# A bridge between two stages: the first expert's last tokens go through their first product between the steps of the earlier tokens' second product

## The chip, the cores and the metric

The kernel runs on 1 core of one Trainium2 chip. The metric is the device time of one execution in microseconds; less is better. Three timed runs of the kernel before gave a median of 729.29 us (727.39 to 729.51).

## What is computed

Attention with a cluster mask (4 batches, 8 heads, 768 positions, head size 64), and then a mixture of 16 experts (4 groups of 4) over the 3072 tokens of 512 features. Cut to what matters:

```python
def _attn_ref(q, k, v, centroids):
    q_assign = np.argmax(np.einsum('bhsd,hcd->bhsc', q_n, c_n), axis=-1)
    k_assign = np.argmax(np.einsum('bhsd,hcd->bhsc', k_n, c_n), axis=-1)
    mask = q_assign[:, :, :, None] == k_assign[:, :, None, :]
    scores = np.where(mask, scale * np.matmul(q, k.transpose(0, 1, 3, 2)), -1e9)
    ...
    return np.matmul(attn, v)

def _moe_ref(x, w_group, w_expert, w1, w2):
    g_idx = np.argmax(x @ w_group, axis=1)
    ...
            e_idx = np.argmax(xg @ w_expert[g], axis=1)
            ...
            h = np.maximum(xg[mask_e] @ w1[g, e], 0.0)
            ye = h @ w2[g, e]
            out[tok_idx] = combined[:, None] * ye
```

Every expert multiplies its tokens by `w1` (512 x 1024), applies ReLU and multiplies by `w2` (1024 x 512). These are called the first and the second product.

## The kernel before

Values are kept as two fp16 halves, a high one and a low one (names ending in h and l), so that each product is three matmuls: high by high, high by low, low by high.

**Attention** runs batch after batch. The router picks an expert for the tokens of a batch when its attention is done (`Router.decide`), and GpSimd scatters each token's number and weight into a table in DRAM (`table`, L713), six scatters of 128 rows a batch.

**Experts** run in order of their number of tokens. The expert that leads after three batches is "the first expert"; its weights are fetched and split while attention still runs (`WA`). Its tokens come in two parts. Part A, up to 288 tokens of the first three batches, is gathered and transposed during the last heads (`xTA`), and is computed by the generator `ga` (`part_a`): 8 steps of the first product, then 8 steps of the second, each of 12 matmuls of 288 columns. Part B, up to 128 tokens of the last batch, is known only after the last `decide`. Beside A's steps the kernel

- makes the tables of the last batch on VectorE (`slots_new`, a generator in several steps, whose one-hot rows `oS` lie in a tile named `hh`; its last step, `widths`, makes `wi`, two words that say which experts may run with fewer columns),
- picks B's rows out of the attention output by a product with a one-hot matrix (`tokens_b`, L1288 and L1292; the result is `xT`, evicted by VectorE and ScalarE at L1289),
- computes every expert's list of token numbers and weights with two groups of matmuls (`slots`, L1306 and L1312), copies them to `ri` and `rg` (L1142, L1143), and starts the first gathers: GpSimd fetches rows of `xbuf` by `ri` into `xg` (L995), three gathers for the next expert, and three for the one behind it that follow at once on GpSimd's queue.

Then `ranks` runs one round for each expert, `k = -1, 0, 1, ...`. Round `k` interleaves, in 8 steps, the first product of expert `k` with the second product of the one before. Round -1 is B's first product (L1036, 128 columns), with nothing of a second product beside it, since A's is over by then. In its middle the tokens of expert 0 are transposed on TensorE (`tokens`, L1005, evicted to `xT` at L1007), and A's result is turned back and written (`settle`, L1114 and L1127, scatter L1128).

**Weights** of the later experts stream in by SyncE in chunks of 512 KB (`st`, L810). A chunk is split in two steps: ScalarE (later by turns GpSimd) makes the high half (L817, `wh..`), VectorE the low half (L820, `wl..`). `next(self.fill)` takes one chunk a step. A chunk's buffer comes free, and the next load can start, when its low half is made.

**Order.** Rounds 0 to 14 are traced in a block with a bound order (`manual_schedule(engines=PINNED)`): TensorE, ScalarE and VectorE execute in the order in which the code is written. Everything ahead of them, round -1 too, is ordered by the scheduler, with `issue_after` as a hint. Part of the code before:

```python
    for i, _ in enumerate(ga):
        with tc.issue_after(X.mm.ins):
            if i >= X.ADD:
                next(new, None)
            if i == X.SLOTS:
                X.slots()
            if i == X.SLT:
                X.xTB = X.tokens_b()
```

PSUM banks: three for the first product (`psh`), two for the second (`psy`), three for everything else (`psm`). A PSUM tile's bank comes free when its eviction is done: `hh` by ScalarE (L1040) and `hl` by VectorE (L1041) for a `psh` tile, `yh` (L1070) and `yl` (L1071) for a `psy` tile of A.

## Time and profile before

| | |
|---|---|
| median of 3 runs | 729.29 us (727.39 to 729.51) |
| profiled execution | 725.85 us, of which the span is 724.1 us |
| TensorE (PE) busy | 690.4 us, 95% of the span |
| VectorE (DVE) busy | 594.9 us, 82% |
| GpSimd (POOL) busy | 498.1 us, 69% |
| ScalarE (ACT) busy | 478.3 us, 66% |
| mean granted TensorE clock | 0.990 |

The span runs from the first to the last instruction of one profiled execution. Attention takes the time up to about 391 us, the stretch that the change rewrites lies between 404.5 and 440.0 us, and the rounds of the later experts follow. PE is matmuls, PEld weight loads, which overlap them. A row of the timeline gives start, duration, engine, line, operation, output and inputs, count, and in brackets the idle time of the engine just before with what ended it. "remote" there means a semaphore whose writer the profile could not name at that moment, "issue" that the row shows no wait.

### The profile page before, as it was taken

To read this page: it belongs to the slowest core of one execution; us is meant where nothing else is said; L and a number is where in the kernel's file an instruction comes from. 1 tells how busy PE (TensorE), PEld (TensorE's weight loads), DVE (VectorE), ACT (ScalarE), POOL (GpSimd) and SP (SyncE) were. 2 spreads that over 40 slices of the span, in tenths; PEclk is the share of its full clock that TensorE was granted. 3 is DMA by queue.
4 is the path that set the end of the run, shared out by engine and by line. 5 is a ranking of instruction groups with operands and counts; after the bars stand their busy time and mean duration, and the time that the engine had idled before them with its cause. 6 is when DMAs were issued, how large, how long until landed. Compare 5 with 4: busy or idle time off the path is not lost.

```text
span 724.1 us, 26359 instructions
## 1 busy us (share of the span) xinstructions
PE 690.4 (95%) x10520; PEld 587.5 (81%) x10520; DVE 594.9 (82%) x1228; ACT 478.3 (66%) x921; POOL 498.1 (69%) x538
## 2 busy tenths in 40 slices
PE   5889999999999999999999979999999999999996
PEld 3667888887788878878778767888779989999996
DVE  5999989899898998989896737878678787999961
ACT  5658798897988979887994246545444554555542
POOL 9777898889988899889973333644645464665433
PEclk9999999999999999999999989999999999999998
DMA  9866727558275573633835468887979797889831
GB/s 252 203 171 170 205 73 200 133 125 196 75 202 135 133 187 80 135 90 78 202 74 106 76 196 316 291 221 240 323 238 309 256 306 248 293 285 318 289 103 51
DMA packets 91848, 137.27 MB, mean 190 GB/s; under 512 B 43815, under 2 KB 61735, under 8 KB 91704
## 3 DMA queue, kind: packets, MB, share of 16 engines
q1 hardware_dynamic: 85948, 121.81, 60.2%
q0 software_dynamic: 5600, 13.40, 5.3%
q8 instruction: 103, 1.69, 1.0%
q14 instruction: 41, 0.34, 0.2%
q10 hardware_dynamic: 156, 0.03, 0.0%
HBM read 93.25 MB, written 14.11 MB: 148 GB/s over the span
## 4 chain that ended last, share of the span: by engine, by line
PE 69%; DVE 12%; ACT 8%; issue 5%; DMA 3%; POOL 1%; another core or an unknown queue 1%; SPq 1%; POOLq 0%; DVEq 0%; ACTq 0%
PE psh L1036 19%; PE psy L1064 14%; PE pso L394 9%; PE psc L320 6%; PE psf L362 5%; PE psf L363 5%; DVE mpart L323 5%; PE psy L1088 4%; ACT p L367 3%; PE psm L253 2%; PE psm L1114 2%; PE psm L1005 1%; ACT ph L371 1%; DMA qx<-xbuf,idA 1%; PE psm L632 1%
## 5 line engine op out<-in xcount | busy, mean ns | idle before, releaser
L374 POOL TENSOR_TENSOR pl<-p 128x512 f16<-128x512 f32 x193 | 198.3, 1052 | 19.5 <-ACT p L367 17.1
L323 DVE TENSOR_REDUCE mpart<-psc 128x1 f32<-128x512 f32 (+1 forms) x282 | 188.2, 680 | 17.5 <-PE psc L320 15.7
L367 ACT ACTIVATE p<-psf 128x512 f32<-128x512 f32 x288 | 171.6, 599 | 40.6 <-PE psf L363 31.0
L394 PE MATMUL pso<-V,pl 128*128 128x65 f16 (+1 forms) x1968 | 160.7, 193 | 0.0
L362 PE MATMUL psf<-A 82*128 82x384 f16 (+2 forms) x576 | 143.7, 274 | 2.4 <-ACT p L367 0.8
L363 PE MATMUL psf<-B 128*128 128x384 f16 (+2 forms) x576 | 143.6, 274 | 0.0
L394 PEld LDWEIGHTS <-pl 128*128 128x128 f16 x1968 | 130.8, 97 | 1.9 <-issue 0.4
L394 PEld LDWEIGHTS <-p 128*128 128x128 bf16 x1632 | 112.5, 98 | 20.3 <-issue 0.5
L394 PE MATMUL pso<-V,p 128*128 128x65 f16 x1632 | 120.8, 193 | 0.0
L374 POOL TENSOR_TENSOR pl<-p,ph 128x512 f16<-128x512 f32 x84 | 96.7, 1160 | 24.8 <-POOL pl L374 9.5
L320 PE MATMUL psc<-A 80*128 80x512 f16 (+1 forms) x376 | 106.8, 328 | 4.6 <-DVE mpart L323 3.2
L1040 ACT ACTIVATE hh<-psh 128x160 f16<-128x160 f32 (+14 forms) x136 | 47.1, 346 | 88.4 <-PE psh L1036 78.6
L1041 DVE SCALAR_TENSOR_TENSOR hl<-psh,hh 128x160 f16<-128x160 f32 (+14 forms) x136 | 50.4, 371 | 54.2 <-ACT hh L1040 44.1
L995 POOL DMA_INDIRECT xg<-xbuf,ri x32 | 37.3, 1167 | 57.0 <-PE psm L1005 28.9
L1036 PE MATMUL psh<-xT,wh0a 128*128 128x288 f16 (+12 forms) x512 | 69.2, 247 | 1.3 <-DVE yl L1071 1.2
L363 PEld LDWEIGHTS <-B 128*128 128x128 f16 x576 | 56.8, 99 | 13.8 <-issue 4.2
L362 PEld LDWEIGHTS <-A 82*128 82x128 f16 x576 | 56.0, 98 | 9.5 <-issue 0.9
L1036 PE MATMUL psh<-xT,wh0b 128*128 128x272 f16 (+6 forms) x448 | 60.7, 247 | 0.1
L1036 PE MATMUL psh<-xT,wl0a 128*128 128x288 f16 (+7 forms) x256 | 60.1, 246 | 0.3 <-issue 0.3
L1128 POOL DMA_INDIRECT out_dram<-y,ri x32 | 36.7, 1148 | 24.7 <-ACT y L1127 17.7
L1036 PE MATMUL psh<-xT,wl0b 128*128 128x248 f16 (+6 forms) x224 | 53.7, 246 | 0.0
L371 ACT CAST ph<-p 128x512 f16<-128x512 f32 x84 | 51.9, 617 | 2.3
(316 smaller groups left out, 1650.9 us busy)
## 6 DMA issues: line engine op xcount, KB each, us to landing
st<-w SPq DMA_DIRECT2D x128, 512.0 KB
B<-parts SPq DMA_DIRECT2D x64, 192.0 KB
kx<-kT SPq DMA_DIRECT2D x16, 384.0 KB
qx<-qT SPq DMA_DIRECT2D x16, 384.0 KB
vx<-vr SPq DMA_DIRECT2D x16, 384.0 KB
A<-parts SPq DMA_DIRECT2D x32, 192.0 KB
xbuf<-xs SPq DMA_DIRECT2D x16, 384.0 KB
A<-mk SPq DMA_DIRECT2D x56, 24.0 KB
```

Source lines behind the costliest of these rows:

```text
L320: last["mm"] = nc.tensor.matmul(out=pc[:, off:off + k1 - k0], lhsT=QA[h % 8][0:80, c * P:(c + 1) * P], rhs=KA[h % 8][0:80, k0:k1], start=T ...
L323: nc.vector.tensor_reduce(out=(mp[:, 0, 0:1], mp[:, :, 1], mp[:, 1, 0:1])[i], in_=pc.rearrange("p (a x) -> p a x", a=n), axis=AX.X, op=ALU ...
L362: nc.tensor.matmul(out=o, lhsT=KA[h % 8][0:82, ks], rhs=QA[h % 8][0:82, q0:q1], start=True, stop=False)
L363: nc.tensor.matmul(out=o, lhsT=KBs[h][:, ks], rhs=QBs[h][:, q0:q1], start=False, stop=True)
L367: cfg["exp"] = nc.scalar.activation(out=p32, in_=pf, func=AF.Exp, scale=QK / (SQ * SQ))
L371: nc.scalar.copy(out=ph, in_=p32)
L374: lo = (nc.vector if u in (EARLY if h < 2 else DVE_LO[h % 8] if h < NH - 2 else DVE_END[h - NH]) else nc.gpsimd).tensor_tensor(out=pl, in0 ...
L394: nc.tensor.matmul(out=O[:, col:col + v.shape[-1]], lhsT=p[:, bs], rhs=v, start=c == 0 and q == 0 and i == 0, stop=c == NCH - 1 and i == l ...
L1036: self.mm = nc.tensor.matmul(out=ph[:, 0:n], lhsT=w[:, k, fs], rhs=xT[:, a, k, 0:n], start=i == 0, stop=i == 3 * KD - 1)
L1040: nc.scalar.activation(out=hh[:, f], in_=ph[:, 0:M], func=AF.Relu)
L1041: self.ev = nc.vector.scalar_tensor_tensor(out=hl[:, f], in0=ph[:, 0:M], scalar=0.0, in1=hh[:, f], op0=ALU.max, op1=ALU.subtract)
L1064: self.mm = nc.tensor.matmul(out=py[:, 0:n], lhsT=w[:, f, d * P:(d + 1) * P], rhs=a[:, f, 0:n], start=i == 0, stop=i == len(prods) - 1)
```

## The change

A new method `bridge` takes the place of the loop above and of round -1. A's 8 steps of the first product run as before. From the second product on, everything is traced inside a bound block:

- `tokens_b` comes after A's first step of the second product (it was after its fifth), `slots` after its third (it was after its sixth).
- B's first product has its 8 steps spread by `BESIDE`: of A's eight steps of the second product, counted from 0, steps 1, 3, 4, 5, 6 and 7 are each followed by one step of B's, and the last two of B's stand behind the transposes of expert 0's tokens.
- A's results are turned back (`settle`) at the very end of the bridge, behind B's last step.
- one weight chunk is taken with each step from `slots` on, eight in all, as many as before.
- `oS` lies in the memory of `wh1b`, the not yet filled high half of expert 0's second weights, and no longer in a tile named `hh`.
- `ranks` starts at round 0 with the state that `bridge` returns.

The core of the diff:

```diff
-    SLOTS = 13
-    SLT = 12
+    SLOTS = 2
+    BESIDE = 0, 1, 0, 1, 1, 1, 1, 1
...
-        self.oS = self.xp.tile([P, T, max(self.caps)], F16, name="hh")
+        n = T * max(self.caps)
+        self.oS = self.W[1][1][0].rearrange("p f d -> p (f d)")[:, 0:n].rearrange("p (t x) -> p t x", t=T)
...
+    def bridge(self, ga, new):
+
+        for i in range(8):
+            next(ga)
+            with self.tc.issue_after(self.mm.ins):
+                if i >= self.ADD:
+                    next(new, None)
+        self.pinned = True
+        with self.tc.manual_schedule(engines=PINNED):
+            h = []
+            up = None
+            for i in range(8):
+                next(ga)
+                if self.left:
+                    self.left()
+                    self.left = None
+                for _ in range((2, 1, 0, 1)[i] if i < 4 else 0):
+                    next(new, None)
+                if i == 0:
+                    self.xTB = self.tokens_b()
+                    up = self.up(self.xTB, P, self.WA[0:2], h)
+                for _ in range(self.BESIDE[i]):
+                    next(up)
+                if i == self.SLOTS:
+                    self.slots()
+                if i >= self.SLOTS:
+                    next(self.fill)
+            for _ in ga:
+                pass
+            xT = self.tokens(self.xg0, self.caps[0])
+            for _ in up:
+                next(self.fill)
+            self.settle()
+        return xT, self.xg0, None, self.down(h, P, self.WA[2:4], [self.gB], [self.idB])
...
-                for _ in range((1, 1, 1, 0, 0, 2, 2, 1)[i] if k < 0 else 1):
-                    with ExitStack() as order:
-                        for op in (self.kept, self.turned, self.got, self.yev[min(1 + i, 3)], self.ev) if k < 0 else (self.ev,):
-                            order.enter_context(self.tc.issue_after(op.ins))
-                        next(self.fill, None)
+                with self.tc.issue_after(self.ev.ins):
+                    next(self.fill, None)
...
-        state = round_(-1, xT, xgs, nxt, down)
-        self.pinned = True
...
+    state = X.bridge(ga, X.slots_new())
```

How the change moves instructions is seen at three places. Lines behind L940 have numbers lower by 1 in the changed kernel up to L1208, so L1041 there is L1040.

**ScalarE, from A's second product on.** `yh` (128x288) evicts a tile of A's second product, `hh` (128x128) one of B's first product, `wh0a` and `wh0b` are weight chunks of experts 0 and 1. Before:

```order
L1070 ACTIVATE yh<-psy 128x288 x2
L1289 CAST xT<-psm 128x512
L817 ACTIVATE wh0a<-st 128x2x512
L1070 ACTIVATE yh<-psy 128x288
L817 ACTIVATE wh0a<-st 128x2x512
L1070 ACTIVATE yh<-psy 128x288
L817 ACTIVATE wh0a<-st 128x2x512
L1040 ACTIVATE hh<-psh 128x128
L817 ACTIVATE wh0a<-st 128x2x512
L1040 ACTIVATE hh<-psh 128x128 x2
```

Of the change:

```order
L1289 CAST xT<-psm 128x512
L1069 ACTIVATE yh<-psy 128x288
L1039 ACTIVATE hh<-psh 128x128
L817 ACTIVATE wh0a<-st 128x2x512
L1069 ACTIVATE yh<-psy 128x288
L1039 ACTIVATE hh<-psh 128x128
L817 ACTIVATE wh0a<-st 128x2x512
L1039 ACTIVATE hh<-psh 128x128
L817 ACTIVATE wh0a<-st 128x2x512
L1069 ACTIVATE yh<-psy 128x288
L1039 ACTIVATE hh<-psh 128x128
```

The four evictions of A's second product stood ahead of all of B's; now they stand between them, and `tokens_b`'s eviction is the first of all.

**VectorE, ahead of expert 0's tokens.** `hl` (128x128) evicts B's first product, `wl..` are the low halves of weight chunks, `xT` (128x4x128) are expert 0's transposed tokens. Before:

```order
L820 SCALAR_TENSOR_TENSOR wl0a<-st,wh0a 128x2x512
L1041 SCALAR_TENSOR_TENSOR hl<-psh,hh 128x128 x3
L1007 COPY xT<-psm 128x4x128 x2
L1007 COPY xT<-psm 128x4x32
L820 SCALAR_TENSOR_TENSOR wl0a<-st,wh0a 128x2x512
```

Of the change:

```order
L1040 SCALAR_TENSOR_TENSOR hl<-psh,hh 128x128
L820 SCALAR_TENSOR_TENSOR wl0a<-st,wh0a 128x2x512
L1070 SCALAR_TENSOR_TENSOR yl<-psy,yh 128x288
L1040 SCALAR_TENSOR_TENSOR hl<-psh,hh 128x128
L820 SCALAR_TENSOR_TENSOR wl0a<-st,wh0a 128x2x512
L1040 SCALAR_TENSOR_TENSOR hl<-psh,hh 128x128
L820 SCALAR_TENSOR_TENSOR wl0a<-st,wh0a 128x2x512
L1070 SCALAR_TENSOR_TENSOR yl<-psy,yh 128x288
L1040 SCALAR_TENSOR_TENSOR hl<-psh,hh 128x128
L820 SCALAR_TENSOR_TENSOR wl0b<-st,wh0b 128x2x512
L1006 COPY xT<-psm 128x4x128 x2
L1006 COPY xT<-psm 128x4x32
```

Three low halves of chunks stood ahead of the token copies before; now five do, and a chunk's low half stands right ahead of them.

**TensorE, where the two words of `wi` are read.** `TENSOR_LOAD wi` reads a word into a register of TensorE's sequencer. Before, the first load stood between two steps of B's first product (`wh`, `wl` are `WA`):

```order
L1036 LDWEIGHTS wl_9368
L1036 MATMUL psh<-xT,wl_9368 128x128
L1256 TENSOR_LOAD wi
L1256 ISA x2
L1036 LDWEIGHTS wh_9367
L1036 MATMUL psh<-xT,wh_9367 128x128
```

Of the change, between `settle` (`psm<-back`) and expert 0's first product (`wh0a`):

```order
L1113 LDWEIGHTS yl
L1113 MATMUL psm<-back,yl 32x128
L1256 TENSOR_LOAD wi
L1256 ISA x2
L1256 TENSOR_LOAD wi
L1256 ISA x2
L1267 REGISTER_ALU
L1267 COMPARE_AND_BRANCH
L1035 LDWEIGHTS wh0a
L1035 MATMUL psh<-xT,wh0a 128x288
```

Both loads stand together now, between the last matmul of the bridge and the first of round 0.

## Rows read from the trace of the kernel before

**Rows 1.** The page's first part: busy time of each engine.

```profile
PE 690.4 (95%) x10520; PEld 587.5 (81%) x10520; DVE 594.9 (82%) x1228; ACT 478.3 (66%) x921; POOL 498.1 (69%) x538
```

**Rows 2.** By stretch: length; PE, PEld, DVE, ACT, POOL (instructions); granted clock; DMA share; GB/s.

```profile
404.50:440.00 35.50, 30.32 (x369) 26.10 (x367) 18.08 (x57) 14.48 (x27) 13.62 (x13) 0.90 0.66 176
425.20:431.80 6.60, 2.76 (x48) 2.59 (x46) 2.23 (x5) 2.74 (x5) 3.95 (x5) 0.87 0.69 228
431.80:437.00 5.20, 5.00 (x50) 4.50 (x50) 4.03 (x9) 4.31 (x8) 0.96 (x1) 0.50 0.52 160
```

**Rows 3.** Timeline of TensorE's matmuls: start, duration, engine, line, operation, names, count, idle.

```profile
407.16 1.14 PE L1064 MATMUL psy<-hl,wh 128*128 128x288 f16 x8
...
412.00 1.14 PE L1064 MATMUL psy<-hh,wh 128*128 128x288 f16 x8 [0.56 <-DVE yl L1071]
...
426.31 0.22 PE L1036 MATMUL psh<-xT,wl 128*128 128x128 f16 x1
...
431.85 0.37 PE L1036 MATMUL psh<-xT,wh 128*128 128x128 f16 x2 [3.89 <-issue]
...
433.44 0.39 PE L1036 MATMUL psh<-xT,wh 128*128 128x128 f16 x2 [0.16 <-issue]
...
440.00 0.42 PE L1036 MATMUL psh<-xT,wh0a 128*128 128x288 f16 x2
```

**Rows 4.** Timeline of ScalarE.

```profile
411.05 0.84 ACT L1070 ACTIVATE yh<-psy 128x288 f16<-128x288 f32 x2 [5.04 <-remote]
...
431.19 0.28 ACT L1040 ACTIVATE hh<-psh 128x128 f16<-128x128 f32 x1 [3.50 <-remote]
...
436.25 0.59 ACT L1007 COPY xT<-psm 128x512 f16<-128x512 f16 x1
```

**Rows 5.** Timeline of GpSimd: the last table scatter of six, and three gathers of six.

```profile
409.29 0.96 POOL L713 DMA_INDIRECT table<-pay,rdi  x1 [0.30 <-issue]
423.26 0.98 POOL L995 DMA_INDIRECT xg<-xbuf,ri  x1 [13.02 <-issue]
...
427.01 0.95 POOL L995 DMA_INDIRECT xg<-xbuf,ri  x1 [0.31 <-issue]
...
429.51 0.86 POOL L995 DMA_INDIRECT xg<-xbuf,ri  x1 [0.30 <-issue]
```

**Rows 6.** The chain that ended last, 380 to 450 us: start, duration, what.

```profile
422.14 3.05 PE psy L1064 x24
...
438.02 1.45 PE psm L1114 x24
```

**Rows 7.** Timeline of VectorE.

```profile
422.18 0.21 DVE L1142 CAST ri<-psm 128x48 int32<-128x48 f32 x1 [2.15 <-PE psm L1312]
...
425.67 0.46 DVE L1071 SCALAR_TENSOR_TENSOR yl<-psy,yh 128x288 f16<-128x288 f32 x1 [3.17 <-ACT yh L1070]
...
426.99 1.27 DVE L820 SCALAR_TENSOR_TENSOR wl0a<-st,wh0a 128x1024 f16<-128x1024 f32 x1
...
431.71 1.22 DVE L820 SCALAR_TENSOR_TENSOR wl0a<-st,wh0a 128x1024 f16<-128x1024 f32 x1
432.85 0.28 DVE L1041 SCALAR_TENSOR_TENSOR hl<-psh,hh 128x128 f16<-128x128 f32 x1
433.05 1.22 DVE L820 SCALAR_TENSOR_TENSOR wl0a<-st,wh0a 128x1024 f16<-128x1024 f32 x1
...
435.79 0.43 DVE L1007 COPY xT<-psm 128x512 f16<-128x512 f16 x1 [0.25 <-PE psm L1005]
```

**Rows 8.** Line L1256 on TensorE's sequencer: min/median/max ns, first and last start.

```profile
L1256 PEldq EVENT_SEMAPHORE  x6: 51/51/51, 431.9 to 432.4; - x6
L1256 PEldq TENSOR_LOAD <-wi x2: 318/404/489, 432.5 to 438.9; - x2
```

**Rows 9.** The DMA queue's own waits, 440 to 560 us, and the stretch 640 to 680.

```profile
SPq L810 <- DVE wl0b L820: 25.1, 12, 5.6
...
640.00:680.00 40.00, 40.00 (x576) 39.58 (x574) 38.47 (x59) 23.97 (x53) 25.10 (x25) 1.00 0.90 310
```

More of the change, by code (lines that the diff above doesn't have):

```diff
@@ L937, in open @@
         self.xp = ctx.enter_context(tc.tile_pool(name="mxp", bufs=2))
-        self.yev = []
         self.pinned, self.left = False, None
@@ L1069, in leave @@
                 def leave(d=d, py=py):
-                    self.yev.append(nc.scalar.activation(out=yh[:, d, 0:M], in_=py[:, 0:M], func=AF.Copy, scale=1.0 / YS))
+                    nc.scalar.activation(out=yh[:, d, 0:M], in_=py[:, 0:M], func=AF.Copy, scale=1.0 / YS)
                     nc.vector.scalar_tensor_tensor(out=yl[:, d, 0:M], in0=py[:, 0:M], scalar=1.0 / YS, in1=yh[:, d, 0:M], op0=ALU.mult, op1=ALU.subtract)
@@ L1401, in turned_tokens, with ranks @@
         return xT.rearrange("p k a m -> p a k m")[:, :, :, 0:self.caps[r]]
-    def ranks(self, bg):
+    def bridge(self, ga, new):
[31 more added lines that the diff above has]
+        return xT, self.xg0, None, self.down(h, P, self.WA[2:4], [self.gB], [self.idB])
+    def ranks(self, bg, state):
         E, sizes = self.R.E, self.sizes
-        xT, xgs, nxt, down = self.xTB, self.xg0, None, iter(())
         def round_(k, xT, xgs, nxt, down):
             nT = None
-            M = self.caps[k] if k >= 0 else P
-            if 0 <= k < E - 2:
+            M = self.caps[k]
+            if k < E - 2:
                 xgs = nxt or self.gathers(k + 1)
@@ L1413, in round_ @@
             h = []
-            up = self.up(xT, M, self.weights_of(k, 0) if k >= 0 else self.WA[0:2], h, k if k >= 0 else None)
+            up = self.up(xT, M, self.weights_of(k, 0), h, k)
             for i in range(8):
-                while k >= 0 and self.ready < 4 * k + (4 if i >= 4 else 2) or k > 0 and self.ready2 < 4 * k - 4 + (4 if i >= 4 or not self.feature_major(self.caps[k - 1]) else 2):
+                while self.ready < 4 * k + (4 if i >= 4 else 2) or k > 0 and self.ready2 < 4 * k - 4 + (4 if i >= 4 or not self.feature_major(self.caps[k - 1]) else 2):
                     next(self.fill)
@@ L1419, in round_ @@
                 next(down, None)
-                if i == (self.SETTLE if k >= 0 else 6):
+                if i == self.SETTLE:
                     self.settle()
@@ L1440, in round_ @@
             xT = nT
-            if k >= 0:
-                cols = [(self.gates[0:m, t, k:k + 1], self.ids[0:m, t, k:k + 1]) for t, m in enumerate(sizes[k])]
-                down = self.down(h, M, self.weights_of(k, 1), [g for g, _ in cols], [i for _, i in cols], k)
-            else:
-                down = self.down(h, M, self.WA[2:4], [self.gB], [self.idB])
+            cols = [(self.gates[0:m, t, k:k + 1], self.ids[0:m, t, k:k + 1]) for t, m in enumerate(sizes[k])]
+            down = self.down(h, M, self.weights_of(k, 1), [g for g, _ in cols], [i for _, i in cols], k)
             return xT, xgs, nxt, down
-        state = round_(-1, xT, xgs, nxt, down)
-        self.pinned = True
         with self.tc.manual_schedule(engines=PINNED):
@@ L1606, in tile_cluster_attention_moe @@
     X.slots_b()
-    new = X.slots_new()
-    for i, _ in enumerate(ga):
-        with tc.issue_after(X.mm.ins):
-            if i >= X.ADD:
-                next(new, None)
-            if i == X.SLOTS:
-                X.slots()
-            if i == X.SLT:
-                X.xTB = X.tokens_b()
+    state = X.bridge(ga, X.slots_new())
     def late():
@@ L1621, in late @@
         yield
-    X.ranks(late())
+    X.ranks(late(), state)
     fix.run()
```

## The prediction

> **What bounds the kernel now.** The page's shares come first: TensorE is busy for 690.4 us, 95% of the span, with VectorE next at 82% [rows 1]. An average over stages says little about one of them, so the stretch that the change rewrites is looked at by windows. In 404.5 to 440.0 TensorE is busy for 30.32 of 35.50 us at a mean granted clock of 0.90; in 425.2 to 431.8 it works for only 2.76 of 6.60 us, and in 431.8 to 437.0 it is busy for 5.00 of 5.20 us at a granted clock of 0.50, the 1.2 GHz level [rows 2]. So the bridge loses 35.50 - 30.32 = 5.2 us to idle time and up to 2.5 us to the clock. TensorE's timeline puts the idle time in places: 0.56 us before the tile at 412.00, and 3.89 us before 431.85 [rows 3]. The reader is to see that these two holes, and not the amount of work, are what a new order can win.
>
> Why they are there is read from the evictions. ScalarE evicts A's first second-product tile only at 411.05, after 5.04 us of waiting on "remote", though that tile's last matmuls ended at 407.16 + 1.14 = 408.30; it evicts B's second tile at 431.19 after 3.50 us on "remote", though the last matmul of that step ended at 426.31 + 0.22 = 426.53 [rows 3, 4]. With all three `psh` banks waiting for evictions, TensorE stands. GpSimd is what both waits have in common: six indirect DMAs back to back, whose last issue ends at 410.25 in one case and at 430.37 in the other, 0.80 and 0.82 us before the evictions start [rows 4, 5]. I read it thus: while GpSimd issues a chain of indirect DMAs, TensorE's finish signals reach ScalarE late, and come through some 0.8 us after the chain's end. It does not bite at once: A's tile of the chain's first 2 us (422.14 + 3.05 = 425.19, where the chain began at 423.26) was evicted in time for VectorE's low half at 425.67 [rows 5 to 7]. The first step held ended 3.27 us after the chain began.
>
> **The change, part by part.**
>
> *Slots earlier.* Before, six of A's second-product steps stand ahead of `slots`; now three do. A step is 12 matmuls, 3.05 / 2 = 1.53 us [rows 6], so 4.6 us leave. One step of B comes in ahead: 48 matmuls took 2.76, so 0.69 [rows 2]. The 0.56 us hole goes too, since `tokens_b`, which needs no eviction of A's, now covers the first chain's hold. `ri` and the gathers therefore come 4.6 + 0.56 - 0.69 = 4.5 us earlier, the first gather at 423.26 - 4.5 = 418.8.
>
> *The hold moves with the gathers.* GpSimd's order is unchanged, six gathers in a row. The chain lasts 430.37 - 423.26 = 7.11 us [rows 5], so it ends at 425.9, and the held signals come at 425.9 + 0.82 = 426.7. TensorE no longer stands meanwhile: 36 matmuls of A lie behind the chain's start, between B's. What is held is the evictions, of B's third step (it ends some 3 us after the chain starts, between the 1.9 that passed and the 3.27 that did not) and all that follow. If that one slips through, one `hl` and one low half leave the queue below: 1.3 us earlier.
>
> *VectorE's queue behind the hold.* This is what is late next. By the listing four `hl` of B, four low halves and two `yl` stand behind the held eviction, ahead of the copies of expert 0's tokens. From start to start a low half took 432.85 - 431.71 = 1.14 us and an `hl` 433.05 - 432.85 = 0.20; for a `yl` of 0.46 I take 0.38, less by the same overlap of 0.08 [rows 7]. That is 4 x 0.20 + 4 x 1.14 + 2 x 0.38 = 6.1 us. ScalarE's eviction at 426.7 takes 0.28, so the queue runs from 427.0 to 433.1. Then a token copy on VectorE (0.43) and one on ScalarE (0.59) must clear a `psm` bank before `settle` can start [rows 4, 7]: 434.1. TensorE's matmuls of A, B and the transposes are over by about 431, so about 3 us of idle stand here, in place of the 3.89.
>
> A rule speaks against this part. The gather at 427.01 took 0.95 us beside the low half of 426.99, which has two operands in SBUF; others of the chain took 0.98 and 0.86, so I price low halves beside gathers at nothing [rows 5, 7]. The Trainium skill, "SBUF — State Buffer", section "Who interferes with whom", says that a VectorE instruction with two SBUF inputs contends with a GpSimd instruction that reads SBUF. By it one more low half now beside the chain could lengthen the chain by up to 1.2 us, and the forecast would be 1.2 us later; the trace does not agree in the one place that shows it.
>
> *`settle` and the two words.* `settle` is 24 matmuls, 1.45 us [rows 6], both before and after, but it now stands last. Before, the two reads of `wi` lay one in B's first product, from 431.9 to the next matmul at 433.44 (1.5 us, 0.16 of it a hole), and one after `settle`, from 438.9 to 440.00 (1.1 us) [rows 3, 8]. Now both stand together behind `settle`. The sequencer ran ahead of the array by about 1.0 us (438.9 against the array's end at about 439.96), so from 434.1 + 1.45 - 1.0 = 434.6 they take 2.6 us: expert 0 starts at 437.2. Bounds: if they overlap wholly, at `settle`'s end, 435.6; if they only start when the array is empty, 435.6 + 2.6 = 438.2.
>
> *At nothing:* `oS` in the memory of `wh1b` (the same instructions, and ScalarE fills that half only near the bridge's end; without that cover the fill would wait for `slots`, which is 15 us earlier); the eight fills, as many as before; the last-batch tables, needed by `slots` and made on VectorE during `tokens_b`, with about 2 us in hand as I lay the queue out. SyncE gets chunk buffers back earlier, never later, as the first low half is made around 421.5 and no longer at 426.99 [rows 7].
>
> *Sum.* 440.0 - 437.2 = 2.8 us off. The later rounds are paced by TensorE, so it should last to the end. The profiled execution (725.85 us, span 724.1) is 3.44 below the median; the difference is applied to the median: 729.3 - 2.8 = **726.5**. From the bounds above, 725.2 (slip) and 724.9 (reads hidden) to 727.7 (chain longer) make its own range 725.0 to 728.0.
>
> **The rivals.**
>
> *A. The waits on "remote" have another cause* that the new order removes. Then the evictions follow TensorE, VectorE has no queue, and `settle` starts when its matmuls are due, about 431; with 1.45 - 1.0 + 2.6 = 3.0 us expert 0 starts at about 434.1: gain 5.9, **723.4**. For it: the trace never names GpSimd as releaser. Against it: two holds, both ending 0.8 us after a chain [rows 4, 5]. The Trainium skill, "SBUF — State Buffer", "Who interferes with whom", says that TensorE and ScalarE never wait on anyone; by that rule this rival is the right one.
>
> *B. The clock, on the other side.* The 3.89 us hole was followed by 5.2 us at 0.50, and the window with the hole has 0.87, so some 6.9 us were run at the 1.2 GHz level (0.26 x 6.6 = 1.7 and 5.2) [rows 2, 3]. The new order has two holes close together, about 3 us before `settle` and 1.7 after it. If the clock falls in the first, `settle` costs up to 0.5 more on the path. If the low stretch of 6.9 us begins at 434.1 it ends at 441.0, and expert 0's first 3.4 us run at half speed, costing 1.7: net gain 0.6, 728.7. If the 6.9 us begin with expert 0 itself, 3.45 + 0.5 are lost: 1.1 slower, **730.4**. It turns to a loss once more than 2 x (2.8 - 0.5) = 4.6 us of round 0 run low. For it: the earlier fall came in a hole not much longer. Against: the holes are shorter, with work between. The Trainium skill, "TensorE: Matmul & The Clock Gate", "What's actually happening", calls the throttled state the default, released by recent activity; the windows agree (0.50 behind the hole), and by it two holes are worse than one.
>
> *C. The gain is made and does not arrive.* In 640 to 680 the DMA share is 0.90 at 310 GB/s, and if the weights limit some round, an earlier start only waits there: **729.3**, with 2.5 either way for chunks that meet other transfers. Against it: the queue waits 25.1 us for low halves in 440 to 560, so compute paces the stream, and TensorE is busy for all of 640 to 680 [rows 9].
>
> **How the numbers follow.** Forecast 0.45, A 0.17, B 0.22, C 0.16. About 0.3% (2.2 us) is what a measurement here can tell from no change: below 727.1 is faster, above 731.5 slower. Of the forecast 0.32 lies below 727.1 and with A 0.17 and C's lower end 0.03 makes 0.52; slower are C's upper end and the worst of B, 0.08; the rest is 0.40. The range takes in A (723.4) and B's loss (730.4): 723.2 to 730.4.
>
> **What would show it.** Gathers from about 418.8 on GpSimd; no hole before 412; ScalarE's wait on "remote" ending near 426.7; VectorE without a gap from 427 to 433; TensorE idle for about 3 us before `settle`, and again before its first matmul on `wh0a` near 437.2 with the two reads there. The forecast is wrong if evictions inside the chain are on time (A), if the granted clock after 434 is 0.50 (B), or if TensorE's later rounds show new waits on low halves or loads (C).

## The result, and the profile after

The changed kernel is slower: 733.86 us (median of 17 runs, 727.57 to 739.09) against 728.39 us for the kernel before (17 runs, 723.89 to 730.39), a ratio of 1.0065 with a 95% interval of 1.0044 to 1.0087. The forecast was 726.5, 0.4% faster, with a range of 723.2 to 730.4.

The profiled execution took 735.66 us (span 733.9), against 725.85 of the one before. Of these 9.8 us, 3.45 were lost before the change begins: A's first product starts at 391.07 in the trace before and at 394.52 in this one, and the granted clock of the first 40 us was 0.70 here against 0.96 (first row before, second row now):

```profile
391.07 0.40 PE L1036 MATMUL psh<-xTA,wh 128*128 128x288 f16 x2 [1.03 <-DMA xTA<-vx]
394.52 0.41 PE L1035 MATMUL psh<-xTA,wh 128*128 128x288 f16 x2 [1.66 <-DMA xTA<-vx]
```

To compare like with like, "the bridge" below is the time from A's first product to expert 0's first matmul. It took 440.00 - 391.07 = 48.93 us before and 446.33 - 394.52 = 51.81 us now, and the stretch behind it 284.1 and 287.6 us.

The page's first part answers to [rows 1], and says as little of single stages as there:

```profile
PE 697.5 (95%) x10520; PEld 592.0 (81%) x10520; DVE 594.6 (81%) x1228; ACT 478.1 (65%) x921; POOL 500.7 (68%) x538
```

By stretch, to be held against [rows 2] (length; PE, PEld, DVE, ACT, POOL; granted clock; DMA share; GB/s):

```profile
409.70:414.00 4.30, 2.00 (x32) 1.76 (x29) 3.17 (x16) 0.00 (x0) 2.57 (x3) 0.94 0.71 21
414.00:423.70 9.70, 9.67 (x59) 8.23 (x60) 2.29 (x6) 1.89 (x4) 0.00 (x0) 0.50 0.90 250
423.70:441.20 17.50, 17.50 (x243) 15.33 (x241) 10.35 (x24) 7.42 (x15) 9.51 (x8) 1.00 0.57 192
441.20:446.30 5.10, 2.04 (x26) 1.42 (x23) 2.72 (x6) 3.85 (x8) 1.32 (x2) 1.00 0.90 333
446.30:460.00 13.70, 13.67 (x80) 8.32 (x81) 6.72 (x9) 6.77 (x11) 3.65 (x3) 0.88 0.75 238
```

TensorE's timeline, answering to [rows 3] (start, duration, engine, line, operation, names, count, idle before):

```profile
409.69 1.73 PE L1288 MATMUL psm<-o,xs 128*128 128x128 f16 x28
412.58 0.27 PE L1288 MATMUL psm<-o,xs 128*128 128x128 f16 x2 [1.16 <-issue]
414.03 2.10 PE L1288 MATMUL psm<-o,xs 128*128 128x128 f16 x18 [1.17 <-issue]
...
432.00 0.22 PE L1035 MATMUL psh<-xT,wl 128*128 128x128 f16 x1
...
441.76 0.22 PE L1113 MATMUL psm<-back,yh 128*128 128x128 f16 x1 [0.48 <-issue]
...
446.33 0.42 PE L1035 MATMUL psh<-xT,wh0a 128*128 128x288 f16 x2 [2.26 <-DMA st<-w]
```

The reader is to see three losses, in order of time. **First**, TensorE stops twice inside the 48 one-hot products of `tokens_b`, 2.3 us in all, where the prediction had put no hole. **Second**, behind that hole it is busy for all of 9.7 us at a granted clock of 0.50, which is 4.85 us of work lost. **Third**, in 441.2 to 446.3 it works for 2.04 of 5.10 us: VectorE's queue and the two reads. Behind expert 0's start the clock is low once more (0.88 over 13.7 us, 1.6 us lost).

GpSimd, ScalarE and VectorE, answering to [rows 4, 5, 7]:

```profile
411.93 0.96 POOL L713 DMA_INDIRECT table<-pay,rdi  x1 [0.30 <-issue]
428.96 0.98 POOL L994 DMA_INDIRECT xg<-xbuf,ri  x1 [16.07 <-issue]
...
432.71 1.56 POOL L994 DMA_INDIRECT xg<-xbuf,ri  x1 [0.30 <-issue]
434.57 1.95 POOL L994 DMA_INDIRECT xg<-xbuf,ri  x1 [0.30 <-issue]
436.82 1.64 POOL L994 DMA_INDIRECT xg<-xbuf,ri  x1 [0.30 <-issue]
```

```profile
433.96 0.28 ACT L1039 ACTIVATE hh<-psh 128x128 f16<-128x128 f32 x1 [2.62 <-PE psy L1063]
```

```profile
414.30 0.69 DVE L1289 CAST xT<-psm 128x512 f16<-128x512 f32 x1 [1.23 <-remote]
...
434.27 0.29 DVE L1040 SCALAR_TENSOR_TENSOR hl<-psh,hh 128x128 f16<-128x128 f32 x1 [0.83 <-issue]
434.48 1.22 DVE L820 SCALAR_TENSOR_TENSOR wl0a<-st,wh0a 128x1024 f16<-128x1024 f32 x1
...
440.67 0.88 DVE L1006 COPY xT<-psm 128x512 f16<-128x512 f16 x3
```

The first gather comes 428.96 - 407.99 = 21.0 us after A's second product begins; the prediction had 418.8 - 404.5 = 14.3. B's third step ended at 432.00 + 0.22 = 432.22 by the matmul rows and was evicted at 433.96, 1.7 us later. VectorE saw TensorE late too: the first half of the one-hot products is 24 of the 48, 28 had run by 409.69 + 1.73 = 411.42, and VectorE evicted that half only at 414.30, after 1.23 us on "remote".

### The profile page after: what moved, and what is told of

Its sections match the earlier page's. It is cut to its first block, busy times and chain, and to the rows that moved or that the text cites. A ratio compares the mean times of both kernels' runs of the same rounds, so it can differ in the third digit from the quotient of the medians.

```text
span 733.9 us, 26357 instructions
## 1 busy us (share of the span) xinstructions
PE 697.5 (95%) x10520; PEld 592.0 (81%) x10520; DVE 594.6 (81%) x1228; ACT 478.1 (65%) x921; POOL 500.7 (68%) x538
## 4 chain that ended last, share of the span: by engine, by line
PE 69%; DVE 13%; ACT 9%; issue 5%; DMA 3%; POOL 1%; SPq 0%; POOLq 0%; ACTq 0%; DVEq 0%
PE psh L1035 18%; PE psy L1063 14%; PE pso L394 9%; PE psc L320 6%; PE psf L362 5%; PE psf L363 5%; DVE mpart L323 5%; PE psy L1087 4%; ACT p L367 3%; PE psm L253 2%; PE psm L1113 1%; PE psm L1004 1%; ACT ph L371 1%; DMA qx<-xbuf,idA 1%; ACT psm L837 1%
## 5 line engine op out<-in xcount | busy, mean ns | idle before, releaser
L367 ACT ACTIVATE p<-psf 128x512 f32<-128x512 f32 x288 | 171.5, 599 | 42.9 <-PE psf L363 32.5
L1039 ACT ACTIVATE hh<-psh 128x160 f16<-128x160 f32 (+14 forms) x136 | 47.1, 346 | 90.4 <-PE psh L1035 79.3
L1040 DVE SCALAR_TENSOR_TENSOR hl<-psh,hh 128x160 f16<-128x160 f32 (+14 forms) x136 | 50.4, 371 | 56.8 <-ACT hh L1039 46.7
L994 POOL DMA_INDIRECT xg<-xbuf,ri x32 | 39.2, 1223 | 57.7 <-PE psm L1004 25.7
L363 PEld LDWEIGHTS <-B 128*128 128x128 f16 x576 | 57.2, 99 | 13.7 <-issue 4.5
L1127 POOL DMA_INDIRECT out_dram<-y,ri x32 | 39.2, 1226 | 23.7 <-ACT y L1126 16.9
```

Source lines behind the costliest of these rows:

```text
L363: nc.tensor.matmul(out=o, lhsT=KBs[h][:, ks], rhs=QBs[h][:, q0:q1], start=False, stop=True)
L367: cfg["exp"] = nc.scalar.activation(out=p32, in_=pf, func=AF.Exp, scale=QK / (SQ * SQ))
L1039: nc.scalar.activation(out=hh[:, f], in_=ph[:, 0:M], func=AF.Relu)
L1040: self.ev = nc.vector.scalar_tensor_tensor(out=hl[:, f], in0=ph[:, 0:M], scalar=0.0, in1=hh[:, f], op0=ALU.max, op1=ALU.subtract)
```

## The experiments

There were eighteen runs of seven kernels, on four chips. The chip matters as much as any edit: on one chip TensorE's finish signals came late beside chains of indirect DMAs, as in the trace before; on the other three no trace shows such a wait, where the kernels were the changed one, its edits, and the kernel before with the scatters late. The kernel before without an edit was traced on the holding chip alone. "The holding chip" and "prompt chips" below are these two sorts. Which chip the first traces of both kernels, before and changed, came from is not on record; their waits and times are those of the holding chip, and they are counted to it. Ratios are to the kernel before on the same chip.

### Scatters late (e1, e6, e9, e13)

The six table scatters of the last batch move out of the bridge, one behind each of rounds 0 to 5. TensorE, VectorE and ScalarE keep their order.

```diff
+            if early:
+                self.held.append(scatter)
+            else:
...
+                if k >= 0 and i == 7 and self.R.held:
+                    with self.tc.issue_after(self.put.ins):
+                        self.R.held.pop(0)()
```

> The changed kernel with the last batch's six table scatters moved out of the bridge, one behind each of rounds 0 to 5; the order on TensorE, VectorE and ScalarE is the same. Theory: these six scatters held TensorE's instruction packet (3.47 us instead of about 0.95), so TensorE stood for 2.3 us inside the one-hot products and then ran at 0.50 for 10 us. Then here there is no hole in the one-hot products, the packet in that stretch takes about 1 us, the granted clock stays 1.00 there, the first gather comes 14 to 15 us after the first matmul of A's second product (21 in the changed kernel), and the time is 3 to 7 us below the changed kernel, about 727 (ratio to before 0.995 to 1.000). Rival 1: the hole is a wait of the one-hot products for something else (a bank, a cast, the buffer of the rows), and the scatters only stand beside it: the hole stays, ratio 1.0065. Rival 2: the clock falls by itself in this order: no hole but 0.50 all the same, ratio about 1.005.

> The changed kernel with the scatters in rounds 0 to 5 (as e1), now beside the changed kernel on one chip. Theory: where signals are held, it is 4 to 7 us below the changed kernel and 1 to 3 below the kernel before, since the holes beside the scatters go and the second chain's hold is covered by A's tiles; where they are prompt, it is within 2 us of the changed kernel. Rival: the scatters only matter through GpSimd's time, and it is the same as the changed kernel on either chip.

> The changed kernel with only the scatters late. Theory, on a chip that holds signals: the holes in the one-hot products and the 0.50 behind them go, the gap before expert 0 (2.3 us, with the reads) stays, the bridge from A's first product to expert 0 takes 46 us (51 to 52 in the changed kernel, 49.0 before, 43.7 with both edits): ratio 0.995 to 0.999. Rival: the reads are what cost there, and the bridge stays above 49 us: ratio above 1.003. On a chip with prompt signals both say 0.997 as in e1 and e6.

> The changed kernel with only the scatters late. Theory, on a chip that holds signals: the holes in the one-hot products and the 0.50 behind them go, the gap before expert 0 stays, the bridge takes about 46 us (50.7 to 52.1 in the changed kernel, 49.0 before, 43.7 with both edits): ratio 0.995 to 0.999. Rival: the reads are what cost there, and the bridge stays above 49 us: ratio above 1.003. On a chip with prompt signals: 0.997 and a bridge of 43 to 44.5 us, as three times before.

Measured: 0.9972 (0.9942 to 1.0002), 0.9976 (0.9947 to 1.0005) and 0.9973 (0.9943 to 1.0003) on the three prompt chips; 0.9950 (0.9923 to 0.9978) on the chip that holds signals, where the changed kernel itself is at 1.008. That last run, e13, is the one that tells. Its trace on TensorE, and by stretch:

```profile
409.10 2.84 PE L1294 MATMUL psm<-o,xs 128*128 128x128 f16 x48
411.78 1.45 PE L1298 MATMUL psm<-pb,st 128*128 128x2 f32 x12
...
435.69 0.22 PE L1119 MATMUL psm<-back,yh 128*32 128x128 f16 x1 [0.79 <-issue]
...
438.42 0.42 PE L1041 MATMUL psh<-xT,wh0a 128*128 128x288 f16 x2 [2.12 <-DMA st<-w]
```

```profile
407.00:424.00 17.00, 16.94 (x225) 14.91 (x224) 9.51 (x41) 4.99 (x9) 2.38 (x3) 1.00 0.57 203
424.00:433.00 9.00, 9.00 (x123) 7.98 (x121) 7.93 (x14) 5.41 (x10) 6.84 (x6) 1.00 0.79 263
```

```profile
421.01 0.99 POOL L1000 DMA_INDIRECT xg<-xbuf,ri  x1 [28.54 <-DMA st<-w]
```

All 48 one-hot products are one row without a hole, the clock stays at 1.00, the first gather comes 421.01 - 407.40 = 13.6 us after A's second product begins, and the bridge takes 44.5 us against 50.7 to 52.1 (about 46 was expected). The gap with the reads (2.12) is still there. So on the holding chip the holes need the scatters beside them, as the theory of e1 has it; the rivals said 1.003 or more. The kernel before with the scatters late did not run on that chip, so how much of the 0.5% is the change's and how much the scatters' is not shown.

### The kernel before, scatters late (e2, e8, e11)

> The kernel before with the same six scatters moved to rounds 0 to 5, nothing else. Theory: before, the work beside the scatters was A's tiles, 24 wide matmuls each with few instructions, so the slow packet was covered; only the 0.50 and 0.56 us holes beside the first chain go, the 3.89 us hole behind the gathers stays: 1 us less, ratio 0.998 to 1.000. Rival: the scatters cost the kernel before as much as they cost the changed one: ratio 0.993 or less, and the change then has no gain of its own.

> The kernel before with the scatters late (as e2), beside the same with the change. Theory: where signals are held, only the 0.5 us holes go and the hole of 3.9 us behind the gathers stays: ratio 0.997 to 1.000, so that with the scatters out of the way the change itself (e6 against this) is worth 1 to 3 us; where they are prompt, the hole is not there at all and the change is worth nothing. Rival: the hole of 3.9 us was due to the scatters too and goes: ratio 0.994 or less on any chip.

> The kernel before with only the scatters late. Theory, on a chip that holds signals: the hole of 3.9 us behind the gathers stays, as it belongs to the second chain; the bridge takes 47.5 to 48.5 us, ratio 0.997 to 1.000, so that the change is worth 1 to 2 us more than this once the scatters are away. Rival: the hole goes, ratio 0.994 or less. On a chip with prompt signals both say 0.998 as in e2 and e8.

The same edit on the kernel before: 0.9978 (0.9948 to 1.0008), 0.9989 (0.9952 to 1.0025) and 0.9986 (0.9951 to 1.0022). All three fell on prompt chips. There the bridge takes 43.4 us in all three traces, and the 3.89 us hole of [rows 3] is not there; TensorE's idle rows of e2 between 398 and 434 are these three:

```profile
427.17 0.27 PE L1042 MATMUL psh<-xT,wh 128*128 128x128 f16 x2 [0.53 <-DVE hl L1047]
...
428.91 0.28 PE L1042 MATMUL psh<-xT,wh 128*128 128x128 f16 x2 [0.91 <-DVE hl L1047]
...
432.35 0.22 PE L1120 MATMUL psm<-back,yh 128*128 128x128 f16 x1 [0.36 <-ACT xT L1013]
```

e2 had expected that hole to stay. I first read this as a hole that the scatters had caused. Against that stand the runs with the scatters in place on prompt chips (c4, e3, e7, e10), where no eviction beside the gathers is late; the kernel before itself has no trace on such a chip.

### Controls: both kernels unedited (c1, c2, c3, c4)

> The changed kernel itself, unedited, as the control for the runs before, with a second trace of it. In the trace of the kernel with the reads early, which has the same order up to the transposes, the packet was just as slow (3.43 us) and there was no hole in the one-hot products. Theory: the hole and the slow clock behind it come in some executions and not in others, and set the spread (727.6 to 739.1 in the first 17 runs); without them the bridge is shorter than before. Then the ratio here lies within 0.996 to 1.008, its spread is wider than that of the kernel with the scatters late (5 us), and the runs with a lower mean clock are the longer ones. Rival: the two reads alone make the difference of 1.2% between this kernel and the one with the reads early: ratio above 1.004 and no overlap of the fastest runs (716.7 there).

> The kernel before, unedited, for a second trace and as a measure of what no change reads like here: ratio 1.000 within its interval. If the 3.89 us hole behind the gathers is of every execution (the first theory of the prediction), it stands in this trace too, at 10 to 11 us after the gathers' start minus 6; if the hold comes and goes, as the kernel with only the scatters moved suggests (no hole behind its gathers), it may be missing here, and then the gain forecast from it was never there in most executions.

> The changed kernel once more, for a third trace: whether the hole in the one-hot products (2.3 us) and the 0.50 behind it are there. Theory: they come and go, so at least one of the two new traces has no such hole, and its bridge is under 46 us; the rival (they belong to the order): both have them.

> The changed kernel as control beside the next three on one chip. The traces so far fall in two sorts: on one chip (e1 to e4) TensorE's finish signals came through during every chain of indirect DMAs, on the other (before, changed, c1 to c3, e5) they were held in every chain, whatever the kernel. Theory: where they are held, this kernel has the holes in the one-hot products and a slow clock behind them and is 0.6 to 0.8% slower than before; where they are prompt, it has neither and is 0.2 to 0.6% faster, as the kernel with the reads early was there. Rival: it is slower on both.

On the holding chip the changed kernel is at 1.008 (1.0048 to 1.0111), and the kernel before against itself at 1.001 (0.9982 to 1.0037). The kernel before has its hole in the second trace as in the first, after the same wait of ScalarE:

```profile
434.11 0.27 PE L1036 MATMUL psh<-xT,wh 128*128 128x128 f16 x2 [3.92 <-issue]
```

```profile
433.45 0.28 ACT L1040 ACTIVATE hh<-psh 128x128 f16<-128x128 f32 x1 [3.53 <-remote]
```

The changed kernel has its holes in all three traces with held signals (2.3, 1.9 and 1.9 us), and the low clock behind them each time, but for different lengths: 10.2, 6.8 and 3.4 us. So the theory of c1 and c3, that the holes come and go on one chip, fell, and c1's rival, a ratio above 1.004, came out. From c1, the holes and the stretches:

```profile
407.35 1.83 PE L1288 MATMUL psm<-o,xs 128*128 128x128 f16 x26
409.65 0.27 PE L1288 MATMUL psm<-o,xs 128*128 128x128 f16 x2 [0.47 <-issue]
410.41 0.22 PE L1288 MATMUL psm<-o,xs 128*128 128x128 f16 x1 [0.49 <-issue]
411.14 0.33 PE L1288 MATMUL psm<-o,xs 128*128 128x128 f16 x3 [0.52 <-issue]
411.90 1.05 PE L1288 MATMUL psm<-o,xs 128*128 128x128 f16 x16 [0.43 <-issue]
412.79 2.51 PE L1292 MATMUL psm<-pb,st 128*128 128x2 f32 x12
```

```profile
407.30:412.90 5.60, 3.64 (x52) 2.96 (x50) 3.84 (x18) 0.00 (x0) 3.20 (x3) 1.00 0.77 22
412.90:419.70 6.80, 6.80 (x39) 5.61 (x39) 1.18 (x4) 1.17 (x4) 0.00 (x0) 0.50 0.93 239
```

On a prompt chip (c4) the same kernel is at 0.9984 (0.9954 to 1.0015), without a hole in the one-hot products; its bridge takes 46.0 us, 1.7 of them the gap with the reads. Expected were a gain of 0.2 to 0.6% and no slow clock. The clock was low twice in that bridge, for 3.4 us each time, once in A's first steps, which the change leaves as they were (the second stretch is shown in the last section):

```profile
390.40:393.80 3.40, 3.37 (x16) 2.19 (x17) 0.56 (x1) 0.17 (x1) 0.00 (x0) 0.51 0.40 120
```

At half clock each of the two costs 1.7 us, an estimate; without them the bridge would take 42.6.

### Reads early (e3, e7, e10, e14)

```diff
+            self.spare(0)
             xT = self.tokens(self.xg0, self.caps[0])
```

The two reads of `wi` stand ahead of the transposes of expert 0's tokens and no longer behind `settle`.

> The changed kernel with the two reads of wi on TensorE's sequencer put ahead of the transposes of expert 0's tokens and no longer behind settle. Theory: behind settle they stand alone for 2.3 us (from the last matmul to the first of expert 0); ahead of the transposes they lie beside queued work, so the gap before expert 0 shrinks to under 0.5 us and the time falls by about 2 us, ratio to before about 1.003 to 1.004. Rival: the gap is a wait for expert 0's weights (the trace names a load of a chunk as what ended it): it stays, ratio 1.0065.

> The changed kernel with the reads of wi ahead of the transposes (as e3), now beside the changed kernel. Theory: the reads are worth the gap before expert 0, 2 to 2.5 us, and no more, on either chip; so if signals are held here, it still has the holes and the slow clock and is at 1.003 to 1.005, against 0.9946 on the first chip. Rival: the reads early also remove the holes (0.995 on any chip).

> The changed kernel with only the reads early. Theory, on a chip that holds signals: holes and slow clock stay, only the gap goes, the bridge takes 48 to 50 us: ratio 1.002 to 1.006. Rival: ratio 0.998 or less. On a chip with prompt signals both say 0.995 to 0.998 as in e3 and e7.

> The changed kernel with only the reads early. Theory, on a chip that holds signals: holes and slow clock stay, only the gap goes, the bridge takes 48 to 50 us: ratio 1.002 to 1.006. Rival: ratio 0.998 or less. On a chip with prompt signals: 0.995 to 0.998 and a bridge of 41.7 us, as three times before.

Measured: 0.9946 (0.9914 to 0.9978), 0.9978 (0.9949 to 1.0006) and 0.9948 (0.9921 to 0.9975) on the prompt chips, with a bridge of 41.7 us three times, the shortest of all; 0.9945 (0.9921 to 0.9969) on the holding chip, where 1.002 to 1.006 was expected. e3 had expected 1.003 to 1.004. The gap before expert 0 is gone in all four, so it was the reads and not the load that its row names; TensorE now stands for 0.7 us ahead of the transposes, as here in e7:

```profile
429.72 1.36 PE L1004 MATMUL psm<-ident,xg 128*128 128x128 f16 x24 [0.74 <-PE psh L1035]
```

On the holding chip the holes are still there (e14):

```profile
413.60 0.27 PE L1288 MATMUL psm<-o,xs 128*128 128x128 f16 x2 [1.15 <-issue]
415.05 1.44 PE L1288 MATMUL psm<-o,xs 128*128 128x128 f16 x18 [1.17 <-issue]
```

Its bridge took 48.1 us, as expected (48 to 50), but the profiled run of 730.84 us is the longest of the kernel's twelve (median 726.23). So the size of the effect of the reads on that chip, 1.3% in the ratios, is not explained by the 2.3 us of the gap, and this trace can't show where the rest went.

The prompt chips tell something else. In e7 ScalarE evicts B's third step at once, 3.3 us after the first gather, where every trace of the change's order on the holding chip has an eviction 1.7 to 3.3 us late (the first row is TensorE's, the last group of that step, 12 matmuls ending at 422.34 + 0.22; then GpSimd's first gather, the eviction, and the 48 one-hot products in one row without a hole):

```profile
422.34 0.22 PE L1035 MATMUL psh<-xT,wl 128*128 128x128 f16 x1
```

```profile
419.29 0.98 POOL L994 DMA_INDIRECT xg<-xbuf,ri  x1 [8.75 <-DMA st<-w]
```

```profile
422.60 0.28 ACT L1039 ACTIVATE hh<-psh 128x128 f16<-128x128 f32 x1 [0.92 <-PE psh L1035]
```

```profile
407.35 2.84 PE L1288 MATMUL psm<-o,xs 128*128 128x128 f16 x48
```

And yet the 16 KB instruction packet beside the scatters was as slow there. It is taken to be TensorE's; the profile gives the queue and not the engine. This is the DMA view of 13 us around the scatters of e7, and behind it that of the changed kernel (queue, packets, MB, share of 16 engines' time):

```profile
q8 instruction: 1, 0.02, 1.6%
...
q8 instruction: 1, 0.02, 1.7%
```

1.6% of 16 x 13 us is 3.3 us for one packet, as on the holding chip (1.7%, 3.5 us); with the scatters late it is 0.6%, 1.2 us, in e13. It was as late, too: by the packets' times it landed 3.8 us after the first one-hot matmul in e7 and 3.9 us in the changed kernel. The theory written for e1, that TensorE stood because its packet was late, therefore falls: a packet that was as late did no harm on a prompt chip. What the holes need is the scatters and a chip that holds signals. One thing more joins the two: in the changed kernel the last scatter's issue ends at 411.93 + 0.96 = 412.89 and the last hole 1.1 us later, and in c1, c3 and e14 it is 0.8, 0.8 and 1.1 us. The prediction had seen held signals come through 0.8 us behind a chain. That hole and hold have one cause is likely by this, and not shown.

### One-hot products late (e4), and both edits (e5, e12)

e4 is the changed kernel with `SLOTS = 3`, `BESIDE = 0, 0, 0, 0, 1, 1, 2, 2` and `tokens_b` after A's fifth step.

> The changed kernel with slots behind A's fourth step and the one-hot products behind its fifth, B's steps after that (one each after the fifth and sixth, two each after the seventh and eighth, two behind the transposes); the scatters stay where they are. Theory: A's wide matmuls now cover the slow packet, so the hole in the one-hot products goes without touching the scatters: time 3 to 8 us below the changed kernel, about 726 to 728 (ratio 0.996 to 1.000). Rival 1 (the hole belongs to the one-hot products): the hole moves with them, ratio above 1.003. Rival 2: the two chains of indirect DMAs now lie close together and the evictions of A's second tile and of B's first steps wait through both: a new hole of 3 us or more, ratio 1.00 to 1.006.

It fell on a prompt chip, where the holes that it was to avoid do not exist: 1.0012 (0.9982 to 1.0042), where 0.996 to 1.000 was expected, and a bridge of 47.1 us. TensorE now waits for a bank that holds the lists and then for a load of weights:

```profile
419.60 1.47 PE L1292 MATMUL psm<-pb,st 128*128 128x2 f32 x12 [2.21 <-DVE rg L1142]
...
422.81 0.28 PE L1035 MATMUL psh<-xT,wh 128*128 128x128 f16 x1 [1.31 <-DMA st<-w]
```

It says nothing on the holes. Whether the change's order of the two is the better one stays open: the intervals of e4 and c4 overlap, and their bridges (47.1 and 46.0) are one trace each, on two chips.

> The changed kernel with both edits: scatters in rounds 0 to 5, reads ahead of the transposes. Theory: the bridge has neither the slow packet nor the gap of 1.7 us that the kernel with late scatters has before expert 0; its bridge, from A's first product to expert 0, is at most that of the kernel with the reads early (41.7 us, 49.0 before), and the time is the lowest of all: ratio to before 0.990 to 0.996. Rival: later rounds take the gain back (the kernel with late scatters lost 5 us there against before with late scatters, with a hole of 2.9 us): ratio 0.997 or more.

> The changed kernel with both edits. Theory: the bridge takes 43 to 44 us on a chip that holds signals and 41 to 42 us where they are prompt (43.5 there for the kernel before with the scatters late), so the ratio is 0.990 to 0.995 on the first sort and 0.995 to 0.998 on the second. Rival: a hole in a later round (that of 4.0 us in the eighth, seen with both edits once) is caused by the scatters in the rounds and takes the gain back on both sorts: 0.998 or more.

Both edits: 0.9932 (0.9905 to 0.9959) on the holding chip, with a bridge of 43.7 us (at most 41.7 was expected), and 0.9985 (0.9950 to 1.0020) on a prompt one, the figure of e12's rival. e5's trace has a hole of 4.0 us in the eighth round, e4's, e1's and c3's one of 2.1 to 2.9 and that of the kernel before one of 1.5, at the same matmuls; what ends it no row shows. e4 and c3 have no scatters in the rounds and the hole all the same, so it does not need them there, as the rival had it; whether they lengthen it is not shown. The expected bridge of 41 to 42 us on the prompt chip was missed: e12's took 45.0. It has two stretches of 3.4 us at the low clock, from 391.4 and from 418.7; take half of them off, as an estimate, and 41.6 are left, the 41.7 of the reads early.

| bridge, us | holding chip | prompt chips |
|---|---|---|
| before | 48.9, 49.0 | not traced |
| before, scatters late | not traced | 43.4, 43.4, 43.4 |
| changed | 51.8, 52.1, 50.7 | 46.0 |
| changed, scatters late | 44.5 | 42.9, 44.6, 42.9 |
| changed, reads early | 48.1 | 41.7, 41.7, 41.7 |
| changed, one-hot products late | not traced | 47.1 |
| changed, both | 43.7 | 45.0 |

## Why the prediction was wrong

**The step that failed** is the one on the 0.56 us hole: "`tokens_b`, which needs no eviction of A's, now covers the first chain's hold". It needs no eviction, and TensorE stops in it all the same: on the holding chip a one-hot stretch of 48 + 12 matmuls takes 2.7 us longer when the scatters stand beside it (the last 12 start 412.79 - 407.35 = 5.4 us after the first matmul in c1, 411.78 - 409.10 = 2.7 in e13). In the order before, A's tiles stood there and ran through the same chain up to 412.00 [rows 3] with one stop of 0.50 us, at 406.06. I had taken "no wait in its operands" for "cannot stop". So the step put the cover of the first chain at no cost, and it cost 2.7 us and the slow clock behind it. Why TensorE stops there, which neither the packet nor any row's releaser explains, stays open.

**What hung on it.** The gathers, forecast 14.3 us after A's second product begins, came after 21.0, 19.7 and 18.0 us in the three traces, and after 13.6 in e13 and e7 where there is no hole: the count of steps was right, the cover was not.

**The clock** was rival B, with 0.22. Its mechanism is what cost most, but the place was another: not the hole before `settle` but the one in the one-hot products starts the low stretch, 10.2, 6.8 and 3.4 us long, 1.7 to 5.1 us lost. In expert 0's first products, where B put it, the clock was low for 3.4 us in two of three traces. With the 2.7 us of the holes that makes 7.8, 6.1 and 4.4 us in the bridge, which is 5.7, 6.0 and 4.6 us longer than the 46.1 (48.9 - 2.8) of the forecast. So the holes and the clock make up the miss in two of the traces, and more than the miss in the first.

**The hold of the second chain** was half right. Signals are held there on this chip, and what is held is B's third step, as said. But it comes through at 5.0, 5.9 and 6.6 us after the chain's start, inside it, and not 0.8 us behind its end (7.9): "until the chain ends" was read from two cases and is wrong. In two of the three traces the hold then came back: in c1, whose gathers begin at 425.33 and end at 433.64, a tile of A that ended at 430.07 was evicted 8.1 us after the start, and c3 is alike with 8.8:

```profile
431.18 0.28 ACT L1039 ACTIVATE hh<-psh 128x128 f16<-128x128 f32 x1 [3.46 <-PE psh L1035]
...
433.42 0.41 ACT L1069 ACTIVATE yh<-psy 128x288 f16<-128x288 f32 x1 [1.02 <-remote]
```

VectorE's queue behind it was right in the changed kernel's trace: 6.4 us from 434.27 to the token copies at 440.67, forecast 6.1. `settle` followed 1.1 us later (1.0), and the reads took 446.33 - 443.6 = 2.7 us (2.6). `settle` itself took 2.3 us with its small holes where 1.45 was taken from [rows 6]. Behind the chain's start lie 48 matmuls of A and not the 36 that the prediction counted; nothing in its sum hung on it.

**The rule on VectorE's second input**, which I priced at nothing, agrees with this trace: three gathers with a low half beside them took 1.56, 1.95 and 1.64 us, and the chain 9.5 us, not 7.1. The Trainium skill, "SBUF — State Buffer", section "Who interferes with whom", has that contention; the one gather of 0.95 in [rows 5, 7], which it does not explain, was too little to set it aside. Here it cost nothing on the path, as the held eviction came at 433.96 and the chain ended at 438.46.

**Rival A** said that the waits on "remote" have another cause than the chains. On the holding chip it is wrong as far as the traces go: the waits stand beside a chain in each, and with the first chain gone (e13) those beside it went. On prompt chips the evictions follow TensorE, as A had it. The rule of the Trainium skill that the prediction put beside A, that TensorE and ScalarE never wait on anyone ("SBUF — State Buffer", "Who interferes with whom"), is about the ports of SBUF; a wait for a signal lies outside it, and these traces speak neither for it nor against it.

**The gain itself.** On a prompt chip the change is at 0.9984 (0.9954 to 1.0015), no difference that can be measured; the hole that it was to fill is not in the kernel before with the scatters late there. With the scatters late its bridge is 43.4 us on the mean (42.9 where the clock did not fall) against 43.4 for the kernel before with the same edit. So as far as the traces show, what the change fills is a hole of one chip, and on that chip it opens a dearer one. On that chip the kernel before itself takes 728.5 to 729.7 us, against 722.3 to 723.1 on the three others.

**What beats the kernel before** is the change with the reads early: 0.9945 to 0.9978 on four chips, with an interval that leaves out 1 on three of them. Beside the changed kernel on a prompt chip (c4 and e7) no difference is shown. How the loss of 0.8% divides on the holding chip stays open: either edit alone recovers it (0.9950 and 0.9945), and both together give 0.9932, so their parts do not add up.

## What to carry to other kernels

A hole's price is not its length: 2.3 us of standing TensorE cost up to 5 us more at half clock, so work that is moved beside a known disturbance must be priced as if it could be stopped, as 48 dense short matmuls were here, with no wait that a row shows. Before an order is rebuilt around a stall, take a second trace on another chip: the stall that this change was made for was seen on one of four. And look for what a new order leaves alone at the end: two register reads of 2.7 us, hidden before, are the cheapest thing to move here.

## What the hardware showed

- One order, two behaviours by chip: on one chip ScalarE evicted tiles of TensorE 1.7 to 4.7 us after their last matmul beside chains of six indirect DMAs (4.7 is 431.19 - 426.53 in the kernel before), and VectorE was late too (414.30 in the changed kernel); on three chips no such wait was seen. The kernel before is 0.7 to 1.0% slower on the first; that the waits make this difference is not shown.
- A 16 KB instruction packet took 3.0 to 3.7 us beside the table scatters and 0.9 to 1.4 in the same stretch without them, on holding and prompt chips alike.
- The clock fell behind `tokens_b` without a hole ahead in c4, e6 and e12, for 3.4 us each, about where the narrow matmuls of `slots` end; in e1 and e9, with the same order there, it did not. In c4 the window with it reads:

```profile
417.00:421.00 4.00, 4.00 (x51) 2.86 (x47) 0.32 (x2) 1.06 (x1) 1.55 (x2) 0.58 1.06 287
```
